# A new plan for a one-core kernel: other assumptions on transfers and small products, and another table of rank amounts

## The chip, the core and the metric

The kernel runs on one NeuronCore of a Trainium2 chip. TensorE (PE) multiplies matrices, VectorE (DVE), ScalarE (ACT) and GpSimd (POOL) work element by element, and SyncE (SP) issues nearly all transfers between the chip's main memory and the core's. Each of these runs its own list of instructions in the order in which they were written, and waits on semaphores where an instruction needs another engine's result. The metric is the device time of one execution in microseconds, the median of three runs.

## What is computed

```python
def reference(**kwargs):
    ...
    attn_out = _attn_ref(**attn_kwargs)
    B, H, S, D = attn_out.shape
    x = np.ascontiguousarray(attn_out.transpose(0, 2, 1, 3)).reshape(B * S, H * D)
    x = _moe_ref(x=x, **moe_kwargs)
    return _moe2_ref(x=x, **moe2_kwargs)

def _attn_ref(r, k, v, w, u):       # batch 4, 8 heads, 768 steps, 48 wide
    for t in range(S):
        kt, vt, rt = (k[:, :, t], v[:, :, t], r[:, :, t])
        cur = np.einsum('bhd,bhe->bhde', u[None] * kt, vt)
        y[:, :, t] = np.einsum('bhd,bhde->bhe', rt, state + cur)
        state = w[None, :, :, None] * state + np.einsum('bhd,bhe->bhde', kt, vt)

def _moe_ref(x, w_in, w_out):       # 3072 tokens, 384 to 2048 to 384
    h = x @ w_in
    sp = np.where(h > 20.0, h, np.log1p(np.exp(np.minimum(h, 20.0))))
    return (h * np.tanh(sp)) @ w_out

def _moe2_ref(x, w_in, w_out, a, b):
    h = x @ w_in
    P = a[0] + a[1] * h + a[2] * h**2 + a[3] * h**3
    Q = 1.0 + np.abs(b[0]) * np.abs(h) + np.abs(b[1]) * h**2
    return (P / (Q + 1e-06)) @ w_out
```

A linear attention with a decaying state is followed by two layers of 384 to 2048 to 384 with an activation between the two products of each.

## The kernel before

The attention is cut into 24 units: 6 chunks of 128 steps for each of 4 batches. A unit (`unit`) loads its keys, receptances and values (`kraw`, `rraw`, `tkv`), multiplies them by powers of the decay `P_T`, and makes a group of small matrix products on PE: the scores (L731), the values (L824, with L818 for the part from the state; L767 in the first two units) and the state's new part (L808; L793 in the first two). In the first four units the diagonal comes from four products two columns wide with the tile `uT` (L708), which holds the input `u`; `uT` is filled by two transfers of single numbers, 0.8 KB each. Two groups (L671) lay out powers of the decay once, and L777 turns the first two units' result round.

Each layer works through 16 slices of 128 features for blocks of 512 tokens. A slice is nine products into a bank `h` (L913), an activation on ACT, DVE and POOL, and nine products into `acc` (L989). A product with 512 columns is full size; the first 24 groups of layer one have 256 columns (half size), so that they may begin when two batches are through the attention. Each value is split into a high and a low part, hence three products for one. Weights come in 64 bits and are brought to 32 bits and split by five or six instructions on ACT, DVE and POOL (L62 to L80, L517, L536).

The order of all this is not written by hand. Everything is recorded as operations in `Plan.ops`, and `Plan.order` makes a list of them when the kernel is built: it keeps a clock for each engine from assumed durations, and picks at each step, among the operations that could start about first, the one of highest rank. A rank is the length of the chain behind an operation plus an amount from the table `PRIO`. Three kinds of assumption bear on the change. A transfer is taken to land `lat` after its last byte, at `move` microseconds of the transfer engines. A group's `rows` says how strongly it is taken to load PE, from which the plan derives the clock that PE is assumed to have. Where the plan finds PE without work in the first 75 us, it puts in fillers: products of zeros into `acc` (L982), which add nothing to the result. They start after eight products of zeros that clear the banks (L650, L978).

Of the kernel before, what the change touches and what calls it, by code (L numbers as in the profile page):

```python
# [18 lines left out]
B, H, S, D = 4, 8, 768, 48  # L19
# [66 lines left out]
def slow_path(tc, nc, d):  # L86
# [133 lines left out]
PRIO = {  # L220
# [32 lines left out]
}  # L253
# [43 lines left out]
class Plan:  # L297
# [72 lines left out]
    def order(self):  # L370
# [14 lines left out]
        for n, x in PRIO.items():  # L385
            self.ops[n].rank += x
        free, clock = {"P": 0.0}, Clock()
        avail = [op for op in self.ops if not op.left]
# [78 lines left out]
def fast_path(tc, nc, d):  # L467
# [3 lines left out]
    pl = Plan()  # L471
# [36 lines left out]
    def dma(dst, src, r=(), w=(), nbytes=196608, after=(), boost=0.0, queue=SP):  # L508

        small = nbytes == 98304  # L510
        return pl.add([(queue, 0.4 if queue != SP else 0.65 if small else 0.5)],
                      lambda e: eng[e].dma_start(out=dst(), in_=src()),
                      r=r, w=w, lat=1.5 if small else 0.757, after=after, move=nbytes / 4.0e5, boost=boost)

# [89 lines left out]
    def setup():  # L604
        dma(lambda: wv(), lambda: d["wT"], w=[wv], nbytes=1000)
        pl.add([(G, 0.1)], lambda e: nc.gpsimd.memset(uT(), 0.0), w=[uT])
        for i in range(2):
            dma(lambda i=i: uT()[64 * i:64 * i + D, :, i], lambda i=i: d["u"].rearrange("(j c) e -> c e j", c=2)[i], w=[uT], nbytes=1000)

# [53 lines left out]
    def powers(after):  # L663

        for i in range(2):
            ps = n_h()

            def ptr(e, i=i, ps=ps):
# [4 lines left out]
                return x_  # L673
            pl.add([(T, 0.9)], ptr, r=[P_T, idn], w=[ps], rows=0.375, after=after)
            pl.add([(A, act(192))],
# [8 lines left out]
    def unit(U):  # L684
# [14 lines left out]
        if U < EARLY:  # L699

            pr = am[0]
            pl.add(mul_opts(512, True), lambda e: eng[e].tensor_tensor(
                out=pr(), in0=kraw(), in1=rraw()[:, :, ::-1], op=ALU.mult), r=[kraw, rraw], w=[pr], boost=bo)
            dp = bank()

            def dsum(e):
                for j in range(4):
                    x_ = nc.tensor.matmul(dp()[:, 2 * j:2 * j + 2], lhsT=pr()[:, j, :], rhs=uT()[:, j, :],  # L708
                                          start=True, stop=True)
                return x_  # L710
            pl.add([(T, 0.75)], dsum, r=[pr, uT], w=[dp], boost=bo, rows=0.2)
            pl.add([(A, 0.2), (V, 0.15)], lambda e: copy(e, dg(), dp()[:, 0:H]), r=[dp], w=[dg], boost=bo)
# [46 lines left out]
        if U < TOK:  # L759
# [3 lines left out]
            def values(e):  # L763
# [5 lines left out]
                return x_  # L769
            pl.add([(T, 1.5)], values, r=[tkv] + am, w=[pv], boost=bo)  # L770
            pl.add([(A, act(384, 0.052)), (V, tt(384), False, VA)],
# [26 lines left out]
        else:  # L798
# [34 lines left out]
            if not last and not join:  # L833
                pl.add([(T, 0.5)], outer, r=[(tkv, 0), (tkv, 1)], w=[kp], boost=bo, rows=0.8)
            xparts = [(xr, i) for i in range(2)]
# [312 lines left out]
```

## Time and profile before

| what | us |
|---|---|
| three runs | 927.40, 928.82, 928.01; median 928.01 |
| profiled execution | 926.85 |
| its span, first to last instruction | 925.1 |
| busy in the span: PE, ACT, DVE, POOL | 908.6, 735.3, 678.9, 525.1 |
| mean granted clock of PE, as a share of 2.4 GHz | 0.989 |

The span is the part of an execution that the profile shows; about 1.8 us of the execution lie outside it. PE busy includes fillers and matmuls that run at the lower clock, so a busy PE is not one that advances at full speed.

### The profile page before, as it was taken

What the parts mean: (1) busy time and instruction counts of PE and PEld (TensorE: products, weight loads), DVE (VectorE), ACT (ScalarE), POOL (GpSimd) and SP (SyncE); (2) the same over time, 40 slices, a digit from 0 to 9 for tenths busy, and PEclk for the clock granted to TensorE, in tenths of its full rate; (3) what the DMA queues carried; (4) which work ended last, traced back from release to release, by engine and by line L of the source; (5) the groups of instructions that cost most, each with busy time, mean ns of one, the idle gap of its engine ahead of it and who ended that gap; (6) DMA issues with size and microseconds to landing.
All of it is one profiled execution on the core that took longest, in us unless ns stands there. A gap on an engine that the chain in (4) does not pass through costs nothing.

```text
span 925.1 us, 14144 instructions
## 1 busy us (share of the span) xinstructions
PE 908.6 (98%) x5094; PEld 750.6 (81%) x5094; DVE 678.9 (73%) x1028; ACT 735.3 (79%) x1310; POOL 525.1 (57%) x468
## 2 busy tenths in 40 slices
PE   7999999999999999999999999999999999999996
PEld 6878778888788888878888888888888888888885
DVE  5699699555545554557868888887877888878894
ACT  4688877767657776769789898997978989878994
POOL 2347747631545421122067597777777876866763
PEclk7899999999999999999999999999999999999999
DMA  8575535230432211117045020020000200100001
GB/s 280 173 262 153 161 122 192 65 123 23 138 95 78 91 46 50 46 49 289 1 140 191 1 68 12 1 69 1 34 24 1 69 12 0 58 1 1 34 1 38
DMA packets 37584, 73.95 MB, mean 80 GB/s; under 512 B 4609, under 2 KB 15746, under 8 KB 37506
## 3 DMA queue, kind: packets, MB, share of 16 engines
q1 hardware_dynamic: 37362, 72.70, 24.1%
q8 instruction: 42, 0.69, 0.3%
q14 instruction: 36, 0.29, 0.1%
q10 hardware_dynamic: 144, 0.26, 0.1%
HBM read 57.61 MB, written 11.01 MB: 74 GB/s over the span
## 4 chain that ended last, share of the span: by engine, by line
PE 91%; DVE 4%; DMA 2%; ACT 2%; issue 1%; POOL 0%; SPq 0%; POOLq 0%; ACTq 0%; DVEq 0%
PE acc L989 41%; PE h L913 32%; PE aps L913 8%; PE aps L731 2%; PE aps L824 2%; PE aps L818 2%; PE acc L982 1%; DVE wr L80 1%; DVE wr L76 1%; DMA uT<-in_u 1%; DMA wr<-in_w 1%; DVE w L536 1%; ACT e L932 1%; PE aps L808 1%; ACT am L748 0%
## 5 line engine op out<-in xcount | busy, mean ns | idle before, releaser
L989 PE MATMUL acc<-gh,w 128*128 128x512 f32 (+1 forms) x1188 | 378.0, 385 | 0.7 <-ACT gh L517 0.7
L913 PE MATMUL h<-xh,w 128*128 128x512 f32 (+1 forms) x960 | 307.0, 384 | 1.8 <-DVE gl L938 1.1
L932 ACT ACTIVATE e<-e 128x512 f32<-128x512 f32 (+1 forms) x408 | 238.1, 602 | 59.1 <-DVE e L928 53.2
L989 PEld LDWEIGHTS acc<-gh,w 128*128 128x128 f32 x1188 | 221.5, 188 | 46.2 <-ACT gh L517 1.1
L989 PE MATMUL acc<-gl,w 128*128 128x512 f32 (+1 forms) x594 | 228.0, 384 | 0.3 <-DVE gl L938 0.2
L913 PEld LDWEIGHTS h<-xh,w 128*128 128x128 f32 x960 | 178.6, 188 | 39.1 <-DVE gl L938 1.1
L913 PE MATMUL h<-xl,w 128*128 128x512 f32 (+1 forms) x480 | 183.4, 382 | 0.4 <-DVE xl L536 0.4
L951 POOL TENSOR_TENSOR v<-v,x 128x512 f32<-128x512 f32 x96 | 124.2, 1300 | 41.7 <-ACT v L945 38.1
L536 POOL TENSOR_TENSOR gl<-yy,gh 128x512 fp32r<-128x512 f32 x94 | 121.7, 1299 | 26.8 <-ACT gh L517 22.2
L989 PEld LDWEIGHTS acc<-gl,w 128*128 128x128 f32 x594 | 111.7, 188 | 22.3 <-DVE gl L938 0.8
L934 DVE SCALAR_TENSOR_TENSOR h<-e,h 128x512 f32<-128x512 f32 (+1 forms) x102 | 67.3, 660 | 57.5 <-ACT e L932 57.3
L913 PEld LDWEIGHTS h<-xl,w 128*128 128x128 f32 x480 | 90.3, 188 | 17.5 <-DVE xl L536 0.6
L928 DVE TENSOR_SCALAR e<-h 128x512 f32<-128x512 f32 (+1 forms) x102 | 66.9, 656 | 48.5 <-PE h L913 48.2
L938 DVE TENSOR_TENSOR gl<-h,gh 128x512 fp32r<-128x512 f32 (+1 forms) x102 | 66.8, 655 | 31.1 <-ACT gh L517 30.1
L517 ACT ACTIVATE gh<-h 128x512 fp32r<-128x512 f32 (+1 forms) x99 | 55.7, 564 | 31.4 <-DVE h L934 31.0
L953 ACT ACTIVATE x<-v,ceps 128x512 f32<-128x512 f32 x96 | 69.0, 723 | 14.1 <-POOL v L951 14.0
L945 ACT ACTIVATE v<-x,cf 128x512 f32<-128x512 f32 x96 | 77.6, 816 | 0.3
L913 PE MATMUL aps<-xh,w 128*128 128x512 f32 x228 | 75.1, 390 | 0.0
L715 POOL TENSOR_TENSOR kraw<-kraw,P_T 128x512 f32<-128x512 f32 x19 | 26.7, 1406 | 55.3 <-DMA kraw<-in_kT 55.3
L963 DVE SCALAR_TENSOR_TENSOR v<-v,ceps,h 128x512 f32<-128x512 f32 x58 | 43.0, 745 | 16.7 <-ACT h L961 16.4
L955 DVE TENSOR_TENSOR yy<-yy,h 128x512 f32<-128x512 f32 x58 | 39.7, 686 | 20.9 <-ACT yy L948 18.8
L913 PEld LDWEIGHTS aps<-xh,w 128*128 128x128 f32 x228 | 42.8, 188 | 8.8
(136 smaller groups left out, 1358.6 us busy)
## 6 DMA issues: line engine op xcount, KB each, us to landing
wr<-in_w SPq DMA_DIRECT2D x32, 768.0 KB, 5.1
tkv<-in_tkv SPq DMA_DIRECT2D x24, 384.0 KB, 3.2
rraw<-in_rT SPq DMA_DIRECT2D x24, 256.0 KB, 3.6
kraw<-in_kT SPq DMA_DIRECT2D x24, 256.0 KB, 2.7
x<-o SPq DMA_DIRECT2D x24, 256.0 KB, 2.3
o<-x SPq DMA_DIRECT2D x24, 256.0 KB, 3.0
out_x<-o SPq DMA_DIRECT2D x17, 256.0 KB, 2.3
xr<-y SPq DMA_DIRECT2D x44, 96.0 KB, 3.4
```

The lines of the kernel that those rows point to most:

```text
L517: return nc.scalar.activation(out=out, in_=x, func=AF.Copy)
L536: lambda e: eng[e].tensor_tensor(out=lo(), in0=x(), in1=hi().bitcast(F32), op=ALU.subtract),
L913: x_ = nc.tensor.matmul(h()[:, :n], lhsT=w()[:, a, m, :], rhs=x()[:, m, col:col + n], start=(i == 0), stop=(i == 8))
L928: pl.add([(V, tt(n))], lambda e: nc.vector.tensor_scalar(out=es(), in0=hp(), scalar1=20.0, scalar2=None, op0=ALU.min), r=[h], w=[e_])
L932: lambda e, func=func, kw=kw: nc.scalar.activation(out=es(), in_=es(), func=func, **kw), w=[e_])
L934: lambda e: nc.vector.scalar_tensor_tensor(out=hp(), in0=es(), scalar=-0.5, in1=hp(), op0=ALU.add, op1=ALU.mult), r=[e_], w=[h])
L938: lambda e: nc.vector.tensor_tensor(out=gls(), in0=hp(), in1=ghs().bitcast(F32), op=ALU.subtract),
L945: lambda e: nc.scalar.activation(out=v(), in_=x(), func=AF.Identity, scale=cf()[:, 5:6], bias=cf()[:, 4:5]), r=[x, cf], w=[v])
L951: lambda e: eng[e].tensor_tensor(out=v(), in0=v(), in1=x(), op=ALU.mult), r=[x], w=[v])
L953: lambda e: nc.scalar.activation(out=x(), in_=v(), func=AF.Ln, bias=ceps()), r=[v, ceps], w=[x])
L963: lambda e: nc.vector.scalar_tensor_tensor(out=v(), in0=v(), scalar=ceps(), in1=h(), op0=ALU.add, op1=ALU.mult), r=[h, ceps], w=[v])
L989: x_ = nc.tensor.matmul(ac[m]()[:, col:col + n], lhsT=w()[:, a, 3 + m, :], rhs=x()[:, :n], start=(first and i == 0 and s > 0), stop=(final ...
```

## The change

The table `PRIO` is replaced: it held other amounts, and now has 409 entries. Six assumptions in the planner are altered: the transfer engines are taken as occupied until 1.8 us, a transfer lands later (`lat` 1.1 for 0.757, and 1.6 for 1.5 on the 96 KB ones) and moves at 0.39 MB per us for 0.4, each half of `uT` counts as 80,000 bytes for 1,000, and five kinds of small product have another duration or load PE less. Nothing else is altered; all products, transfers and element-wise operations are those of before, and only the order, the choice of engine where an operation has one, and the number of fillers differ. Lines after the table stand seven lines further down (L708 is L715, L982 is L989, and L989 is L996).

```diff
--- before.py
+++ after.py
@@ -218,38 +218,45 @@
 PRIO = {
-    21: 17, 29: -1, 31: 384, 39: -30, 41: -150, 43: -213, 53: -152, 54: 84, 56: -56, 59: -47, 60: -2, 66: -8, 67: -5,
...
+    15: 13, 28: -62, 31: -45, 46: 257, 54: -44, 55: -26, 56: -192, 64: -49, 79: 18, 82: -69, 120: -7, 127: -9,
...
@@ -384,7 +391,7 @@
             op.rank = op.boost + max([c + 0.15 + x.rank - x.boost for x in op.succ + places[op]] + [t + x.rank for x, t in op.chain], default=c)
         for n, x in PRIO.items():
             self.ops[n].rank += x
-        free, clock = {"P": 0.0}, Clock()
+        free, clock = {"P": 0.0, "dma": 1.8}, Clock()
         avail = [op for op in self.ops if not op.left]
         order = []
         while avail:
@@ -510,7 +517,7 @@
         small = nbytes == 98304
         return pl.add([(queue, 0.4 if queue != SP else 0.65 if small else 0.5)],
                       lambda e: eng[e].dma_start(out=dst(), in_=src()),
-                      r=r, w=w, lat=1.5 if small else 0.757, after=after, move=nbytes / 4.0e5, boost=boost)
+                      r=r, w=w, lat=1.6 if small else 1.1, after=after, move=nbytes / 3.9e5, boost=boost)
 
     def copy(e, out, x):
         if e == A:
@@ -605,7 +612,7 @@
         dma(lambda: wv(), lambda: d["wT"], w=[wv], nbytes=1000)
         pl.add([(G, 0.1)], lambda e: nc.gpsimd.memset(uT(), 0.0), w=[uT])
         for i in range(2):
-            dma(lambda i=i: uT()[64 * i:64 * i + D, :, i], lambda i=i: d["u"].rearrange("(j c) e -> c e j", c=2)[i], w=[uT], nbytes=1000)
+            dma(lambda i=i: uT()[64 * i:64 * i + D, :, i], lambda i=i: d["u"].rearrange("(j c) e -> c e j", c=2)[i], w=[uT], nbytes=80000)
 
         def small(fn, r, w, e=V, c=0.1):
             pl.add([(e, c)], fn, r=r, w=w)
@@ -671,7 +678,7 @@
                     x_ = nc.tensor.matmul(ps()[:, j * D:(j + 1) * D], lhsT=P_T()[rows, j, :], rhs=idn()[rows],
                                           start=True, stop=True)
                 return x_
-            pl.add([(T, 0.9)], ptr, r=[P_T, idn], w=[ps], rows=0.375, after=after)
+            pl.add([(T, 0.9)], ptr, r=[P_T, idn], w=[ps], rows=0.2, after=after)
             pl.add([(A, act(192))],
                    lambda e, i=i, ps=ps: copy(A, P_t().rearrange("p (j c e) -> p c j e", j=4, c=2)[:, i],
                                               ps()[:, 0:192].rearrange("p (j e) -> p j e", j=4)),
@@ -708,7 +715,7 @@
                     x_ = nc.tensor.matmul(dp()[:, 2 * j:2 * j + 2], lhsT=pr()[:, j, :], rhs=uT()[:, j, :],
                                           start=True, stop=True)
                 return x_
-            pl.add([(T, 0.75)], dsum, r=[pr, uT], w=[dp], boost=bo, rows=0.2)
+            pl.add([(T, 0.75)], dsum, r=[pr, uT], w=[dp], boost=bo, rows=0.05)
             pl.add([(A, 0.2), (V, 0.15)], lambda e: copy(e, dg(), dp()[:, 0:H]), r=[dp], w=[dg], boost=bo)
         ps = [bank(), bank()]
         for x in (kraw, rraw):
@@ -767,7 +774,7 @@
                         x_ = nc.tensor.matmul(pv()[:, h * D:(h + 1) * D], lhsT=am[i]()[:, j, :],
                                               rhs=tkv()[:, 384 + h * D:384 + (h + 1) * D], start=True, stop=True)
                 return x_
-            pl.add([(T, 1.5)], values, r=[tkv] + am, w=[pv], boost=bo)
+            pl.add([(T, 1.6)], values, r=[tkv] + am, w=[pv], boost=bo, rows=0.4)
             pl.add([(A, act(384, 0.052)), (V, tt(384), False, VA)],
                    lambda e: copy(e, yt().rearrange("p (c e j) -> p j c e", c=2, j=4),
                                   pv()[:, 0:384].rearrange("p (j c e) -> p j c e", j=4, c=2)), r=[pv], w=[yt], boost=bo)
@@ -831,7 +838,7 @@
             pl.add([(A, act(512, 0.052)), (V, tt(512), False, VA)],
                    lambda e: copy(e, y()[:, :, :CH], pv().rearrange("p (h t) -> p h t", h=4)), r=[pv], w=[y], boost=bo)
             if not last and not join:
-                pl.add([(T, 0.5)], outer, r=[(tkv, 0), (tkv, 1)], w=[kp], boost=bo, rows=0.8)
+                pl.add([(T, 0.5)], outer, r=[(tkv, 0), (tkv, 1)], w=[kp], boost=bo, rows=0.5)
             xparts = [(xr, i) for i in range(2)]
             for i in range(2):
```

On SP, the first transfers of the program (12 of them, an input's name behind the arrow), before:

```order
L512 DMA tkv<-in_tkv 128x768
L512 DMA wv<-in_wT 128x4
L512 DMA rraw<-in_rT 128x512
L512 DMA kraw<-in_kT 128x512 x2
L512 DMA uT<-in_u 48x4x1
L512 DMA rraw<-in_rT 128x512
L512 DMA wr<-in_w 128x1536
L512 DMA uT<-in_u 48x4x1
L512 DMA wr<-in_w 128x1536 x3
```

and with the change (the first 11):

```order
L519 DMA wv<-in_wT 128x4
L519 DMA uT<-in_u 48x4x1
L519 DMA kraw<-in_kT 128x512
L519 DMA rraw<-in_rT 128x512
L519 DMA wr<-in_w 128x1536
L519 DMA uT<-in_u 48x4x1
L519 DMA rraw<-in_rT 128x512
L519 DMA tkv<-in_tkv 128x768
L519 DMA kraw<-in_kT 128x512
L519 DMA wr<-in_w 128x1536 x2
```

The two transfers of `uT` were the sixth and the ninth, the second of them behind 2,176 KB of others; they are now the second and the sixth, the second behind 1,280 KB. The first keys and receptances move ahead of the first `tkv`.

On PE, from the last products of zeros to the first scores (`aps` and `h` are banks, `acc` the accumulators), before:

```order
L978 MATMUL acc_159<-zer 128x512
L978 MATMUL acc_161<-zer 128x512
L978 MATMUL acc_163<-zer 128x512
L982 MATMUL acc_159<-zer 128x512 x7
L708 MATMUL aps_94<-uT,am 128x2 x4
L982 MATMUL acc_159<-zer 128x512 x2
L731 MATMUL aps_95<-rraw,kraw 128x128
```

and with the change, where three clearings and four fillers stand ahead of these rows:

```order
L657 MATMUL aps_94<-zer 128x512
L657 MATMUL aps_95<-zer 128x512
L657 MATMUL h_96<-zer 128x512
L657 MATMUL h_97<-zer 128x512
L657 MATMUL h_98<-zer 128x512
L989 MATMUL acc_137<-zer 128x512 x11
L715 MATMUL aps_94<-uT,am 128x2 x4
L989 MATMUL acc_137<-zer 128x512 x2
L738 MATMUL aps_95<-rraw,kraw 128x128
```

Between the clearings and the first L708 group (now L715) there were 7 fillers and are 15; the two after it remain.

On PE, from the first unit's values on (two score groups and more stand around this piece), before:

```order
L767 MATMUL aps_95<-tkv,am 128x48 x8
L982 MATMUL acc_159<-zer 128x512 x4
L777 MATMUL aps_94<-idt,tr 128x128 x3
L793 MATMUL aps_95<-tkv 48x48 x8
L982 MATMUL acc_159<-zer 128x512 x2
L767 MATMUL h_98<-tkv,am 128x48 x8
L982 MATMUL acc_159<-zer 128x512
L708 MATMUL aps_94<-uT,am 128x2 x4
L777 MATMUL h_96<-idt,tr 128x128 x3
L793 MATMUL h_97<-tkv 48x48 x8
```

and with the change, from the first turned result to the third score group, and then from the second turned result on:

```order
L784 MATMUL aps_94<-idt,tr 128x128 x3
L800 MATMUL aps_95<-tkv 48x48 x8
L989 MATMUL acc_137<-zer 128x512
L715 MATMUL aps_94<-uT,am 128x2 x4
L774 MATMUL h_98<-tkv,am 128x48 x8
L738 MATMUL aps_95<-rraw,kraw 128x128
```

```order
L784 MATMUL h_96<-idt,tr 128x128 x3
L800 MATMUL h_97<-tkv 48x48 x8
L831 MATMUL aps_95<-am,tkv 48x128 x8
L920 MATMUL h_98<-xh,w 128x256
L920 MATMUL h_98<-xl,w 128x256
L920 MATMUL h_98<-xh,w 128x256 x2
L920 MATMUL h_98<-xl,w 128x256
L920 MATMUL h_98<-xh,w 128x256 x2
L920 MATMUL h_98<-xl,w 128x256
L920 MATMUL h_98<-xh,w 128x256
L815 MATMUL aps_94<-tkv 48x48 x8
L715 MATMUL aps_95<-uT,am 128x2 x4
```

Before, 45 fillers stand behind the first scores: 10 up to the second L767 group and its neighbours, 5 ahead of the first half-size L913 group, and 30 between that and the sixth. With the change 6 stand there: one in the piece shown, two after the third half-size L913 group (now L920), and three single ones. Between the first scores and the first half-size group PE now runs three score groups, L671, two L708 groups, two L767, two L777, two L793 and one L824 with one filler among them.

## Rows read from the trace of the kernel before

**Rows 1.** The page: busy time with share, and PE's granted clock by slice.

```profile
PE 908.6 (98%) x5094; PEld 750.6 (81%) x5094; DVE 678.9 (73%) x1028; ACT 735.3 (79%) x1310; POOL 525.1 (57%) x468
...
PEclk7899999999999999999999999999999999999999
```

**Rows 2.** Stretches: length, busy time (instructions) of each engine, PE's clock, transfers.

```profile
0.00:10.00 10.00, 5.55 (x15) 4.09 (x15) 3.81 (x21) 1.28 (x1) 2.19 (x15) 1.00 0.78 238
10.00:13.00 3.00, 1.73 (x12) 1.40 (x14) 2.63 (x4) 1.53 (x4) 0.88 (x1) 1.00 1.01 416
13.00:30.30 17.30, 17.30 (x102) 15.51 (x101) 9.45 (x16) 11.65 (x27) 3.20 (x3) 0.51 0.59 197
30.30:64.10 33.80, 32.18 (x316) 27.55 (x314) 29.85 (x44) 24.97 (x59) 16.24 (x12) 1.00 0.71 236
64.10:100.00 35.90, 34.87 (x370) 31.25 (x370) 32.69 (x54) 29.69 (x79) 24.40 (x21) 1.00 0.65 200
140.00:918.00 778.00, 778.00 (x4065) 639.21 (x4063) 567.12 (x846) 633.24 (x1085) 453.76 (x395) 1.00 0.18 59
918.00:925.10 7.10, 0.18 (x1) 0.00 (x0) 0.23 (x1) 0.60 (x1) 0.00 (x0) 0.71 0.34 120
```

**Rows 3.** PE's waits: for what, us in total, times, longest.

```profile
PE aps L708 <- DMA uT<-in_u: 3.5, 1, 3.5
...
PE h L913 <- DVE gl L938: 1.1, 2, 0.5
...
PE acc L989 <- DVE gl L938: 0.2, 1, 0.2
```

**Rows 4.** Fillers alone (L982), in three stretches; columns as in Rows 2.

```profile
13.00:30.30 17.30, 4.09 (x8) 2.46 (x9) 0.51 0.59 197
30.30:36.10 5.80, 0.88 (x3) 0.19 (x1) 1.00 0.67 225
36.10:64.10 28.00, 10.01 (x35) 6.14 (x35) 1.00 0.72 239
```

**Rows 5.** Timeline of PE: start, duration, instruction, count, idle before.

```profile
5.78 1.97 PE L982 MATMUL acc<-zer 128*128 128x512 f32 x7
11.27 1.02 PE L708 MATMUL aps<-uT,am 128*128 128x2 f32 x8 [3.52 <-DMA uT<-in_u]
...
12.80 1.91 PE L731 MATMUL aps<-rraw,kraw 48*128 48x128 f32 x16
14.49 2.67 PE L671 MATMUL h<-idn,P_T 48*128 48x48 f32 x16
17.09 1.86 PE L708 MATMUL h<-uT,am 128*128 128x2 f32 x8
...
20.37 2.08 PE L731 MATMUL h<-rraw,kraw 48*128 48x128 f32 x16
22.38 3.65 PE L767 MATMUL aps<-tkv,am 128*128 128x48 f32 x16
...
29.08 0.88 PE L793 MATMUL aps<-tkv 128*48 128x48 f32 x16
...
30.54 1.88 PE L767 MATMUL h<-tkv,am 128*128 128x48 f32 x16
...
32.56 0.95 PE L708 MATMUL aps<-uT,am 128*128 128x2 f32 x8
...
34.60 0.57 PE L793 MATMUL h<-tkv 128*48 128x48 f32 x16
35.10 1.16 PE L731 MATMUL aps<-rraw,kraw 48*128 48x128 f32 x16
...
43.33 0.28 PE L913 MATMUL h<-xh,w 128*128 128x256 f32 x1
...
44.49 1.16 PE L731 MATMUL aps<-rraw,kraw 48*128 48x128 f32 x16
```

**Rows 6.** The tile uT: time from issue to landing of its two transfers.

```profile
DMA to landing us min/median/max: 5.2/5.8/6.4
```

69 rows, old and new, of the table PRIO are left out of this document.

## The prediction

> **What bounds the kernel now.** I read the page first. PE is busy for 908.6 of 925.1 us, no other engine for more than 735.3, and its granted clock is below full only at the start [rows 1]. So the span is PE's own list, and the question is where PE spends time on something other than this list's useful products. The table of stretches answers it [rows 2]: from 140 to 918 us PE is busy in 778.00 of 778.00 us at full clock, so there a new order can win nothing and can only lose by a wait. After 918 come the last copies and the output, 7.1 us, which stay. What can be won lies ahead of 100 us, and is of four kinds. First, PE has run its first fillers by 7.75 us and then waits 3.52 us, until 11.27, for the second transfer of `uT` [rows 5]. Second, 45 further fillers stand behind the first scores; their busy times are 4.09, 0.88 and 10.01 us in three stretches, 15.0 in all [rows 4]. Third, from 13.0 to 30.3 us PE is busy without a gap, yet at a granted clock of 0.51, that is 1.2 instead of 2.4 GHz [rows 2]. Fourth, PE waits in short pieces: behind the long one of 3.5 us there are seven groups of waits on DVE and ACT from 1.1 down to 0.2 us, 3.9 us together (the first and the last are shown) [rows 3].
>
> **What feeds PE there.** DVE is the fullest engine beside PE: 29.85 of 33.80 us between 30.3 and 64.1, and 32.69 of the next 35.90 [rows 2]. Ahead of 30.3 it is busy for only 3.81 + 2.63 + 9.45 = 15.9 us. So the fillers of the middle stretch mostly stand where DVE was late, and a better order must get DVE to work earlier.
>
> **The change, term by term**, against the profiled execution (span 925.1). The useful products are the same, so only the four kinds count.
>
> *Start, -1.5 us.* In the old order 2,176 KB stand ahead of the second `uT` transfer, in the new one 1,280 KB. The slower of the two took 6.4 us to land [rows 6], and PE went on at 11.27. With 0.59 of the bytes ahead I estimate a landing between 7 and 9 us. PE now has 15 fillers instead of 7 in front of the first L708 group. Seven took 1.97 us from 5.78 on [rows 5]; at full clock one costs 10.01 / 35 = 0.29 us busy [rows 4], about 0.25 without the overlap at a run's end, so eight more end near 7.75 + 2.0 = 9.75. The fillers, not the transfer, then set the group's start, 1.5 us earlier. The bounds are 0 (the transfer lands as late as now) and -1.5.
>
> *Fillers, -11.3 us.* Neighbours overlap a little: the scores that start at 20.37 last 2.08, and the next group starts at 22.38 [rows 5]. Taking about 0.12 us for each of 12 runs, the 45 cost 15.0 - 1.5 = 13.5 us. Six remain. At 0.5 us each at the low clock (4.09 / 8 [rows 4]) and 0.25 at the high one, half of them at either, they cost 2.2. The bounds are -11.3 and 0, the latter if PE waits wherever a filler stood.
>
> *Lower clock, +8.4 us.* This is what the removed fillers may cost. The rows give a price for each group at both clocks [rows 5]: scores 2.08 against 1.16 us, values of the first units (L767) 3.65 against 1.88, L708 1.86 against 0.95, L793 0.88 against 0.57. L671 lasts 2.67 and was seen at the low clock only; at most half of it, 1.3, is the clock's. In the old order the first scores (1.91, so 0.75 too much), L671, one L708, one score, one L767 and one L793 group lie in the slow stretch: 0.75 + 1.3 + 0.91 + 0.92 + 1.77 + 0.31 = 6.0 us. Fillers make up 4.1 of the 17.3 us there [rows 4], and the clock comes back right behind six of them. The new order has one filler there. If the clock falls as before, up to the first half-size L913 group the slow stretch holds L671, two L708, two scores, two L767, two L793 and one L824 (priced as scores): 1.3 + 1.8 + 1.8 + 3.5 + 0.6 + 0.9 = 9.9 us. A half-size group takes 1.16 us at full clock (43.33 to 44.49 [rows 5]); at the low clock I estimate 1.1 more. I take the clock to come back with the third such group, since in the old order it came back behind wide products: 9.9 + 1.1 + 0.3 + 0.9 + 1.1 + 0.9 = 14.2, rounded up to 14.4 for part of the third, 8.4 more than before. The bounds are -6.0 (it never falls) and +16.5 (back only with the second half-size L989 group, by the same prices).
>
> *Short waits, +0.5 us.* By the semaphores of the two orders, 82 DVE instructions had to end before the sixth half-size L913 group, and 78 have to now. DVE's need has not grown, but the cushions are gone. I take 4.4 us for 3.9. The bounds are -3.9 and +8, the latter if most of the removed fillers become waits.
>
> Everything later I cost at nothing: from 140 us on PE covers the other engines, the busiest of which (ACT) has 633 of 778 us [rows 2]; if that cover failed, each wait would add its full length. At the end ten L989 groups follow the last L913 group instead of six, so the last activations have more cover than now.
>
> The sum is -1.5 - 11.3 + 8.4 + 0.5 = -3.9 us: span 921.2, execution 922.9 for 926.85. The median of before lies 1.2 above its profiled execution, so I forecast 928.0 - 3.9 = 924.1.
>
> **A rule against the trace.** The stretch from 13.0 to 30.3 us shows PE without a gap at 0.51 of full clock [rows 2]. The Trainium skill ("TensorE: Matmul & The Clock Gate", Part 1, on the HAM clock gate) says that the throttled state is the default and that activity releases it: a PE kept busy runs at 2.4 GHz. By that, the new order, which keeps PE busy from its first product on, would have no slow stretch behind the start. This would give the first rival below. The trace of before disagrees, since busy with small products was not enough there.
>
> **Rivals.** *The clock holds or comes back early.* For it: with 15 fillers PE no longer idles 3.5 us ahead of the first scores, and the fall at 13.0 followed that idling. Against it: the whole slow stretch was busy. With the clock back by the second L767 group the slow part is 1.3 + 0.9 + 1.8 + 0.9 + 0.3 = 5.2 us, so the term is -0.8 and the sum would be -13. But DVE sets a limit: its 45.7 us of work up to 64.1, plus at least the 6.2 that it idles in the first 10 us and some 3 us of transfers and scores that it must await, put the sixth half-size group no earlier than 55 us. So -9, a median of 919.
>
> *Waits take the fillers' place.* The old fillers stood where PE had nothing to do; if DVE is no earlier, each filler removed turns into idle time, and the lower clock hides it in part. For it: DVE at 0.88 and 0.91 of the two busy stretches. Against it: 18 us of DVE idle ahead of 64 us, 14.4 of them ahead of 30.3. With 3 to 5 us of waits above my term the sum is -1 to +1, a median of 927 to 929.
>
> *The low clock lasts (slower).* Products of 48 and 2 columns and only one wide filler leave PE slow through the half-size groups. The sum is zero at 18.3 us of excess: by the prices above, when the clock comes back only after the fourth half-size L913 group. Back with the second L989 group it is -1.5 - 11.3 + 16.5 + 0.5 = +4.2, a median of 932.
>
> **How the numbers follow.** I give the forecast 0.42, the early clock 0.20, waits for fillers 0.20, the lasting low clock 0.18. About 0.2% (1.9 us) is what a measurement of this kernel can tell from no change. Faster by more: 0.60 (the early clock, and all but 0.02 of the forecast); within it 0.22; slower 0.18. The range 918 to 930.5 leaves out the best of the first rival and most of the last, 0.2 together; the forecast's own range is 921 to 926.
>
> **What would show it.** In the new profile the first L715 group starts near 9.8 us, not 11.3; PE's clock reads 0.5 from about 13 to the low forties; the fillers fall to 23; the sixth half-size L920 group starts near 60 us instead of 64; nothing changes from 140 us on. I am wrong at the first term if the group starts past 10.5, at the third if the clock is full before 30 us or still low at 50, at the fourth if PE's waits on DVE and ACT pass 7 us.

## The result, and the profile after

The changed kernel takes 917.38 us (four runs, 917.02 to 918.55) where the kernel before took 927.96 in runs beside it: a ratio of 0.9882, 95% interval 0.9865 to 0.9898. That is 10.6 us less; 3.9 were forecast, and the range ended at 918. The profiled execution took 917.02 us, 9.8 less than that of before, with a span of 915.2. The page of the new kernel, to set beside [rows 1]:

```profile
PE 902.7 (99%) x5063; PEld 745.5 (81%) x5063; DVE 676.8 (74%) x1025; ACT 726.8 (79%) x1295; POOL 536.8 (59%) x477
...
PEclk7699999999999999999999999999999999999999
```

The stretches of the new kernel, with the columns of [rows 2] (cut at 37.2 and 55.7, where its first and sixth half-size groups begin):

```profile
10.00:13.00 3.00, 3.00 (x36) 2.64 (x36) 1.79 (x3) 1.52 (x6) 2.29 (x2) 1.00 1.02 426
13.00:30.30 17.30, 15.39 (x87) 14.09 (x87) 13.63 (x20) 14.73 (x26) 7.21 (x5) 0.50 0.89 326
30.30:37.20 6.90, 6.90 (x60) 6.20 (x59) 6.90 (x10) 3.06 (x5) 3.35 (x2) 0.52 0.50 175
37.20:55.70 18.50, 18.29 (x215) 16.39 (x214) 17.39 (x30) 16.37 (x41) 13.22 (x11) 1.00 0.79 254
140.00:908.00 768.00, 767.52 (x3968) 629.35 (x3967) 557.62 (x830) 614.86 (x1056) 448.28 (x394) 1.00 0.18 58
```

and two stretches of the kernel before, cut where its first and sixth half-size groups stand (37.4 and 64.0), with the one from the start to the first such group, in the kernel before and then in the new one:

```profile
13.00:37.40 24.40, 24.40 (x171) 22.03 (x170) 13.60 (x22) 14.93 (x35) 6.66 (x6) 0.65 0.63 208
37.40:64.10 26.70, 25.08 (x247) 21.02 (x246) 25.70 (x39) 21.70 (x51) 12.78 (x10) 1.00 0.71 236
0.00:37.40 37.40, 31.68 (x196) 27.51 (x197) 20.03 (x46) 17.74 (x38) 9.73 (x21) 0.77 0.70 233
0.00:37.20 37.20, 33.05 (x206) 29.19 (x206) 27.38 (x53) 21.52 (x38) 15.03 (x23) 0.68 0.78 279
```

The column to read first is the third busy time, DVE's. Both kernels reach the first half-size group at about 37.3 us. On the way DVE did 13.60 us of work in the old one, and 13.63 + 6.90 = 20.53 in the new one; from the start on it is 20.03 and 27.38. Behind it the old one needs 25.70 us of DVE in 26.7 us, all that DVE has; the new one 17.39 in 18.5, and its sixth half-size group starts at 55.65 instead of 64.0. DVE is not alone in this: up to the same point ACT did 21.52 us for 17.74, POOL 15.03 for 9.73, and the transfers ran at 279 GB/s for 233. Part of the work that moved is seen on DVE's timeline. Pieces of layer one's weights (L76, L80, and L543, which was L536) stand in the new kernel at

```profile
15.94 0.96 DVE L76 SCALAR_TENSOR_TENSOR wr<-wr 128x768 int32<-128x768 int32 x1
16.81 1.81 DVE L543 TENSOR_TENSOR w<-wr,w 128x768 fp32r<-128x768 f32 x1
18.54 0.95 DVE L80 SCALAR_TENSOR_TENSOR wr<-wr 128x768 int32<-128x768 int32 x1
```

while the kernel before still has such pieces, 5.6 us in these three rows, at

```profile
49.08 1.76 DVE L76 SCALAR_TENSOR_TENSOR wr<-wr 128x768 int32<-128x768 int32 x1
...
56.32 1.77 DVE L536 TENSOR_TENSOR w<-wr,w 128x768 fp32r<-128x768 f32 x1
58.01 2.05 DVE L80 SCALAR_TENSOR_TENSOR wr<-wr 128x768 int32<-128x768 int32 x1
```

The weights are the smaller part of DVE's lead. Up to the first half-size group its weight pieces take 11.0 us for 8.2 (L73, L76, L80 and L543), its attention pieces 13.7 for 8.7 (L709, L722, L745 and L760: keys, receptances, `tkv`, masks). ACT's two weight steps on the 64-bit values (L62 and L71) take 11.7 us for 6.3.

The new kernel's waits, as in [rows 3], and its fillers alone (L989, columns as in [rows 4]):

```profile
PE h L920 <- DVE w L543: 1.2, 1, 1.2
PE aps L784 <- ACT tr L524: 1.1, 1, 1.1
PE aps L715 <- DVE xl L792: 0.8, 1, 0.8
```

```profile
13.00:36.90 23.90, 0.80 (x1) 0.29 (x1) 0.50 0.78 282
36.90:75.00 38.10, 1.92 (x5) 0.88 (x5) 1.00 0.71 224
```

With three more of 0.2 to 0.3 us, PE's waits behind the start are 3.8 us, for 3.9 before. PE's timeline, as in [rows 5]:

```profile
9.43 0.98 PE L715 MATMUL aps<-uT,am 128*128 128x2 f32 x8
...
11.91 1.73 PE L678 MATMUL h<-idn,P_T 48*128 48x48 f32 x16
13.57 1.86 PE L715 MATMUL h<-uT,am 128*128 128x2 f32 x8
15.29 3.63 PE L774 MATMUL aps<-tkv,am 128*128 128x48 f32 x16
18.85 2.08 PE L738 MATMUL h<-rraw,kraw 48*128 48x128 f32 x16
...
31.32 2.08 PE L738 MATMUL aps<-rraw,kraw 48*128 48x128 f32 x16
...
34.91 0.88 PE L800 MATMUL h<-tkv 128*48 128x48 f32 x16
35.59 1.71 PE L831 MATMUL aps<-am,tkv 128*48 128x128 f32 x16
37.23 0.39 PE L920 MATMUL h<-xh,w 128*128 128x256 f32 x1
...
55.65 0.28 PE L920 MATMUL h<-xh,w 128*128 128x256 f32 x1
```

and the clock around its return:

```profile
36.00:37.00 1.00, 1.00 (x14) 1.00 (x11) 1.00 (x3) 0.00 (x1) 0.00 (x0) 0.57 1.01 391
37.00:38.00 1.00, 1.00 (x12) 0.81 (x8) 1.00 (x2) 1.00 (x2) 0.00 (x0) 1.00 1.11 337
```

The scores, values and L715 groups last as long as at the half clock of [rows 5] (2.08, 3.63, 1.86), up to the L831 group. The L920 group behind them runs at full clock.

### The profile page after: what moved, and what is told of

It reads as the page before. It is cut to its first block, busy times and chain, and to the rows that moved or that the text cites. A ratio compares the mean times of both kernels' runs of the same rounds, so it can differ in the third digit from the quotient of the medians.

```text
span 915.2 us, 14064 instructions
## 1 busy us (share of the span) xinstructions
PE 902.7 (99%) x5063; PEld 745.5 (81%) x5063; DVE 676.8 (74%) x1025; ACT 726.8 (79%) x1295; POOL 536.8 (59%) x477
## 4 chain that ended last, share of the span: by engine, by line
PE 90%; POOL 3%; DVE 2%; ACT 1%; DMA 1%; issue 1%; SPq 0%; POOLq 0%; DVEq 0%; ACTq 0%
PE acc L996 41%; PE h L920 33%; PE aps L920 8%; PE aps L738 3%; PE aps L831 2%; PE aps L825 2%; POOL v L958 1%; DMA wr<-in_w 1%; POOL gl L543 1%; PE acc L989 1%; PE aps L815 1%; DMA xr<-y 1%; PE aps L715 0%; POOL w L543 0%; DVE wr L80 0%
## 5 line engine op out<-in xcount | busy, mean ns | idle before, releaser
L996 PE MATMUL acc<-gh,w 128*128 128x512 f32 (+1 forms) x1188 | 378.3, 385 | 0.0
L920 PE MATMUL h<-xh,w 128*128 128x512 f32 (+1 forms) x960 | 307.6, 384 | 1.5 <-DVE w L543 1.2
L996 PEld LDWEIGHTS acc<-gh,w 128*128 128x128 f32 x1188 | 221.2, 188 | 45.0 <-issue 0.2
L996 PE MATMUL acc<-gl,w 128*128 128x512 f32 (+1 forms) x594 | 228.0, 384 | 0.2 <-POOL gl L543 0.2
L920 PEld LDWEIGHTS h<-xh,w 128*128 128x128 f32 x960 | 178.4, 188 | 38.8 <-DVE w L543 1.4
L920 PE MATMUL h<-xl,w 128*128 128x512 f32 (+1 forms) x480 | 183.1, 381 | 0.0
L543 POOL TENSOR_TENSOR gl<-yy,gh 128x512 fp32r<-128x512 f32 x94 | 121.5, 1298 | 19.0 <-ACT gh L524 15.5
L996 PEld LDWEIGHTS acc<-gl,w 128*128 128x128 f32 x594 | 111.6, 188 | 23.0 <-POOL gl L543 0.9
L920 PEld LDWEIGHTS h<-xl,w 128*128 128x128 f32 x480 | 90.3, 188 | 16.9
L920 PE MATMUL aps<-xh,w 128*128 128x512 f32 x228 | 75.5, 390 | 0.0
L962 DVE TENSOR_TENSOR yy<-yy,h 128x512 f32<-128x512 f32 x58 | 39.8, 685 | 18.0 <-ACT yy L955 10.9
L920 PEld LDWEIGHTS aps<-xh,w 128*128 128x128 f32 x228 | 42.8, 188 | 9.5 <-DVE yy L976 0.6
L728 POOL TENSOR_TENSOR tr<-tr,tkv 128x384 f32<-128x384 f32 x20 | 21.3, 1067 | 45.6 <-DMA tkv<-in_tkv 45.6
```

Of the source, the lines that this page charges most:

```text
L543: lambda e: eng[e].tensor_tensor(out=lo(), in0=x(), in1=hi().bitcast(F32), op=ALU.subtract),
L920: x_ = nc.tensor.matmul(h()[:, :n], lhsT=w()[:, a, m, :], rhs=x()[:, m, col:col + n], start=(i == 0), stop=(i == 8))
L996: x_ = nc.tensor.matmul(ac[m]()[:, col:col + n], lhsT=w()[:, a, 3 + m, :], rhs=x()[:, :n], start=(first and i == 0 and s > 0), stop=(final ...
```

## The experiments

The theory after the first reading: in the old order DVE was late behind 37 us, the fillers stood where PE would have waited for it, and the new order's gain is weight work done by DVE ahead of 37 us, which makes them needless. Rivals: the fillers held PE up by themselves; the start; the clock. Orders below are edited behind the planner, so that all other instructions stay in their places. `k` counts fillers. Each run has one trace, of one of its executions; that execution's time is given where it lies far from the median.

**1. The old order without the 30 fillers.**

```diff
-            (self.fill if op in made else op.fn)(op.eng)
+            k += op in made
+            if op in made and 25 <= k <= 54: continue
+            (self.fill if op in made else op.fn)(op.eng)
```

> The old order, with only the 30 fillers between the first and the sixth half-size L913 group left out; every other instruction stands where it stood, and the result is the same. Theory (the fillers stood where DVE was late): DVE is busy in 25.7 of the 26.7 us of that stretch, so the sixth group still starts near 64, PE now waits some 6 to 8 us on DVE there, and the time is within 1 us of before (927 to 929), a little more if the granted clock falls. Rival (the fillers held PE up by themselves): the sixth group starts near 57 and the time is 920 to 922.

Measured: 928.87, ratio 1.0009 (0.9994 to 1.0025), no gain from some 7 us of products left out. The first half-size group starts at 38.28 in this trace, the sixth at 66.66 instead of 64.0. Its waits and its stretches:

```profile
PE h L913 <- DVE w L536: 2.1, 2, 1.8
PE aps L818 <- DVE am L753: 1.8, 1, 1.8
PE aps L808 <- DVE tkv L738: 1.2, 1, 1.2
```

```profile
44.00:51.00 7.00, 7.00 (x41) 6.37 (x41) 4.68 (x11) 4.53 (x13) 5.19 (x5) 0.51 0.97 349
55.70:64.10 8.40, 4.75 (x44) 3.73 (x42) 8.40 (x11) 5.64 (x11) 4.11 (x3) 0.82 0.71 244
62.00:67.00 5.00, 4.73 (x49) 4.22 (x50) 3.67 (x9) 5.00 (x16) 0.94 (x1) 0.50 0.52 147
```

Waits on DVE took the fillers' place (DVE 8.40 of 8.40 us busy, PE 4.75), and behind those that ended at 41.8 and 62.3 us the granted clock was 0.5 for some microseconds, though PE was busy again. In the old order, then, a filler cost nothing: it stood in for a wait and for a stretch at half clock.

**2. The new order with 26 fillers put back** (`more` names the operations behind which they stand).

```diff
+        made, more = set(), {187: 7, 274: 1, 286: 8, 387: 2, 228: 5, 207: 3}
...
+            for i in range(more.pop(op.n, 0)): self.fill(op.eng)
```

> The new order, with 26 fillers put back between the first and the sixth half-size L920 group, where they stood before. Theory (DVE is ahead there now, so PE alone sets the pace): 26 fillers at 0.25 us are 6.5 us, of which the short waits on DVE and ACT take back 1 to 2: the time is 922 to 924. Rival (DVE or a transfer still sets the pace there): the fillers run in idle time and the time stays at 917 to 918.5.

Measured: 923.47, ratio 0.9953 (0.9936 to 0.9970), 6.1 us above the changed kernel, or 0.23 for each filler; its sixth half-size group starts at 61.70 instead of 55.65. Its stretch of 37.2 to 55.7:

```profile
37.20:55.70 18.50, 18.50 (x175) 16.05 (x172) 13.78 (x27) 14.54 (x34) 11.03 (x10) 0.99 0.75 238
```

In the new order a filler has its full price: PE sets the pace there, and DVE (13.78 of 18.5) has room.

**3. The old order with an early `uT`**: operations 2 and 3, its two transfers, stand right behind operation 1.

```diff
+        made, order = set(), [op for op in self.order() if op.n not in (2, 3)]
+        i = order.index(self.ops[1]) + 1
+        for op in order[:i] + self.ops[2:4] + order[i:]:
```

> The old order, with only the two transfers of uT moved ahead on SP (now the fourth and fifth transfer instead of the sixth and ninth). Theory (the start term of the prediction, and DVE setting the pace from there on): uT has landed by 8 us, the first L708 group starts between 8 and 9.5 instead of 11.27, DVE's work behind it moves with it, and the time is 1.5 to 3 us less (925 to 926.5). Rival (the start is hidden because DVE waits for other things before 37 us): the first group starts earlier, but the first half-size group does not, and the time is within 0.7 us of before.

Measured: ratio 0.9991 (0.9976 to 1.0006). The first group starts at 7.78 instead of 11.27, and yet the first half-size one at 38.05, not ahead of the 37.45 of before:

```profile
7.78 1.02 PE L708 MATMUL aps<-uT,am 128*128 128x2 f32 x8
...
12.27 1.46 PE L731 MATMUL aps<-rraw,kraw 48*128 48x128 f32 x13 [1.72 <-ACT dg L517]
...
38.05 0.28 PE L913 MATMUL h<-xh,w 128*128 128x256 f32 x1
```

The rival's result holds: 3.5 us at the start are gone by 37 us. Its reason holds in part: PE waits 0.7 us for `rraw` and 1.7 for `dg` ahead of the first scores, and then the clock, full there before, reads 0.50 again from 33.2 to 36.6 us. PE's early start alone is worth less than can be measured; the interval leaves room for 2.2 us.

**4. The new table up to operation 599 only**, with the old table's amounts behind and the new assumptions.

```diff
-PRIO = { ... }
+PRIO = {the new amounts of operations below 600, the old ones of all others}
```

> The changed kernel with the new table only for operations numbered below 600 (73 of its amounts: the set-up, the first units and the first half-size slices) and the old table's amounts for all others; the assumptions are the new ones. Theory (all of the gain lies ahead of the sixth half-size group): PE's order is the same up to there, and the time is 917 to 919. Rival (the later amounts contribute): 921 to 925.

Measured: 932.38, ratio 1.0046 (1.0028 to 1.0063): both were wrong, and the kernel is 15 us slower than the changed one. Up to the sixth half-size group it is the changed kernel (55.66 us). It loses in layer two, ahead of the second activation (`yy`):

```profile
PE aps L920 <- DVE yy L976: 5.1, 1, 5.1
PE h L920 <- DVE yy L976: 3.1, 2, 2.8
```

```profile
875.00:880.00 5.00, 1.21 (x6) 0.66 (x4) 4.12 (x7) 4.64 (x8) 3.44 (x4) 0.96 0.00 0
880.00:885.00 5.00, 3.64 (x9) 2.90 (x10) 5.00 (x8) 0.49 (x1) 0.62 (x1) 0.50 0.01 2
```

So the early amounts bring the early gain, and with the old later ones it is lost again: PE waits 8.2 us on `yy`, and the clock is halved behind the wait. I had costed all behind 140 us at nothing. That came out so (767.52 of 768.00 us busy), but ACT's 633 of 778 us, my reason, is none: here ACT is no fuller and PE waits.

**5. The old order, weight pieces early, fewer fillers.** `MOVES` holds 18 pairs; the first of a pair is put ahead of the second in the list. Nine are DVE's, eight ACT's and one SP's (the expectation counts 11 and 6 in error).

```diff
+MOVES = [(80, 48), (98, 48), (104, 48), (81, 254), (85, 254), (86, 254), ...]
...
+        for n, m in MOVES:
+            order.remove(self.ops[n])
+            order.insert(order.index(self.ops[m]), self.ops[n])
+        for op in order:
+            k += op in made
+            if op in made and 25 <= k <= 54: continue
```

> The old order with two edits: 18 instructions of the weights' preparation (11 on DVE, 6 on ACT, 1 transfer) move ahead of instructions at which DVE and ACT idled between 24 and 37 us, and the 30 fillers between the first and the sixth half-size L913 group are left out (as in the run with fewer fillers, which alone gave +1). Theory (the gain is DVE's weight work done in its idle time, which makes the fillers needless): with some 6 us of DVE work gone from the stretch of 37 to 64, the sixth half-size group starts near 58 instead of 64 and the time is 921 to 924. Rival (DVE's lead does not matter, or the clock falls without fillers): 927 to 930.

**6. The same moves with all 54 fillers.**

> The old order with only the first of those two edits: the same 18 instructions earlier, all 54 fillers kept. Theory: PE's own list, the fillers in it, now sets the pace; only the waits of some 2 us between 44 and 64 can go: 925.5 to 927.5. Rival (the gain comes from DVE alone): the same 921 to 924 as with both edits.

Measured: ratios 0.9977 (0.9961 to 0.9993) and 0.9977 (0.9962 to 0.9991), 2.1 us each. The sixth run has the theory's time. PE's waits behind the start fall from 3.9 to 1.4 us; from 37.2 on PE has no gap, and DVE is busy for 12.64 of 18.5 us:

```profile
37.20:55.70 18.50, 18.50 (x188) 16.23 (x184) 12.64 (x24) 14.27 (x36) 9.98 (x9) 0.95 0.71 238
```

From its first to its sixth half-size group it takes 23.95 us (40.75 to 64.70) instead of 26.55; but in this trace the first came 3.3 us later than before, the clock reading 0.50 from 11.8 us on. The fifth run lies between its two ranges: 30 fillers fewer gave nothing more. In its trace, of an execution of 928.16 with a median of 925.84, the sixth group starts at 64.69, not at 58, and one wait stands out (lines stand ten further down here):

```profile
PE h L923 <- DVE gl L948: 4.4, 2, 3.8
```

DVE idled 3.29 us for `gh` there; ACT reached `gh` only after an L62 that had waited 2.54 us for a transfer of weights. So in this execution DVE's queue was not the limit: the next link, the transfers' place on SP, was late too. Where the run's 2.1 us were won, this execution does not show.

**7. The new order with eight fillers more near 21 us** (as in 2, with `more = {62: 8}`).

> The new order, with eight fillers more behind the second score group (near 21 us, in the stretch at half clock). They cost 3.5 us at the half clock, 1 of it in a wait that is there. Theory (from 13 to 37 us DVE, busy for 20.5 of 24 us, sets the pace nearly as much as PE, so the half clock costs far less than its prices): the clock may come back near 25, the first half-size group does not start more than 1 us earlier, and the time is 917 to 919. Rival (the half clock costs what the prices say, some 0.4 us per us at it): the first half-size group starts 2 to 4 us earlier and the time is 913.5 to 915.5. If the clock does not come back: 919 to 920.

Measured: 917.72, ratio 0.9890 (0.9872 to 0.9908), the same as the changed kernel. Its clock:

```profile
20.00:28.00 8.00, 6.14 (x49) 5.02 (x48) 7.58 (x12) 7.57 (x14) 4.92 (x3) 0.93 0.92 328
28.00:38.00 10.00, 9.52 (x66) 8.07 (x66) 10.00 (x13) 6.30 (x10) 3.88 (x3) 0.50 0.65 231
```

In this trace the clock also fell later, at 17.6 us, so it was full for some 10 us more than in the changed kernel's. The first half-size group came 1.1 us earlier, the sixth 0.7, the end not at all. DVE and ACT are busy for 7.58 and 7.57 of the 8 us from 20 on, and PE for 6.14: a faster PE waits there, 1.9 us of it on DVE's `xl`.

**8. The new order with the L80 of 28.0 us done five times.**

```diff
+            for i in range(5 if op.n == 93 else 1): (self.fill if op in made else op.fn)(op.eng)
```

> The new order, with the DVE instruction of 28.0 us (L80, whose result doesn't change when it is repeated) done five times: 3.5 to 3.8 us more of DVE work. Theory (DVE is nearly full from there to 56 us and its lead is what the gain rests on): the groups behind it start 1.5 to 3.5 us later, PE waits on DVE for as much, and the time is 919 to 921. Rival (PE sets the pace alone, DVE has a reserve of several us): less than 1 us, 917 to 918.5.

Measured: 921.59, ratio 0.9939 (0.9916 to 0.9962), 4.2 us more. The five took 5.65 us where one takes 0.95, so 4.7 us of DVE were added, not 3.6. In the trace, of an execution of 923.44, the first half-size group starts at 42.57, 5.3 later, of which 1.2 were lost ahead of the added work; the half clock lasts to 45:

```profile
29.26 5.65 DVE L80 SCALAR_TENSOR_TENSOR wr<-wr 128x768 int32<-128x768 int32 x5
...
30.30:37.20 6.90, 4.87 (x29) 4.49 (x30) 6.80 (x8) 2.62 (x6) 1.08 (x2) 0.50 0.06 22
37.20:45.00 7.80, 6.83 (x53) 5.45 (x53) 7.62 (x10) 4.42 (x8) 3.07 (x3) 0.50 0.69 246
```

What DVE loses between 28 and 37 us the kernel loses nearly in full. With 2 (PE paces behind 37 us) this is the theory's core: DVE up to there, PE from there on. Ahead of 28 us it is not shown. From 13.0 to 30.3 ACT is fuller than DVE in the new kernel (14.73 and 13.63 of 17.3 us), PE's longest wait there is on ACT (`tr`, 1.1 us), and no run made ACT slower.

**9. The old order, 21 moves, fewer fillers.** Sixteen of the pairs of 5, some with a new place, and five more: `(131, 401)`, a weight transfer earlier on SP, `(102, 193)`, `(109, 383)`, `(132, 231)` and `(133, 294)`; `(94, 69)` and `(95, 74)` are left out.

> The old order without the 30 fillers between the first and the sixth half-size L913 group, and with 21 moves instead of the 18 of the earlier run: fewer pieces of the weights stand ahead of what the first half-size group needs, DVE's later pieces of the fourth and fifth weight (L536) move up, so that SP can issue the next weight's transfer earlier, and ACT's step on that transfer (L62) no longer stands ahead of gh. Theory (the gain needs the whole chain of a weight, transfer, ACT and DVE, to be early; the earlier run freed DVE and then waited 3.9 us behind a transfer): the sixth half-size group starts at 58 to 61, and the time is 921 to 924. Rival (in this order something else always takes the fillers' place): 925 to 928.

Measured: ratio 0.9965 (0.9945 to 0.9985), 3.2 us less, at the lower edge of the rival's range. The trace is of an execution of 928.41, with a median of 925.38. In it the sixth group starts at 63.40, not at 58 to 61; the wait behind `gh` is gone, but PE idles 2.4 us on DVE's `tkv`, and the clock falls behind it:

```profile
40.00:42.00 2.00, 0.00 (x0) 0.00 (x0) 2.00 (x4) 1.94 (x5) 0.00 (x0) 1.00 0.12 39
...
44.00:51.00 7.00, 7.00 (x39) 6.55 (x39) 2.80 (x7) 4.49 (x12) 5.17 (x5) 0.50 0.99 394
```

DVE is free there (2.80 of 7.00): in this execution the pieces put forward pushed `tkv` back, and the half clock cost more. A third of the gain could be had by hand; that the remainder is the same cause was not shown by building it up.

**10. The new order without 12 fillers**: seven of the 15 at the start, and the five behind 37 us.

> The new order without 12 of its 23 fillers: seven of the 15 at the start and the five between the first half-size group and 75 us. Theory (PE sets the pace from 37 us on, so the five cost 1.2 us; the seven held the first L715 group up by 1.7 us, but DVE sets the pace behind it, and the old order's run with an early uT gained next to nothing from 3.5 us): 915.5 to 917. Rival (the fillers there hold the clock or fill waits that are there anyway): 917 to 920.

Measured: 918.08, ratio 0.9885 (0.9858 to 0.9912), as the changed kernel. The median is the rival's, but the interval, some 915 to 920 us, does not tell the two ranges apart. In the trace, of an execution of 920.93, the first L715 group waited 1.8 us for `uT`, until 10.40: the transfer had taken 7.1 us to land, where in the changed kernel the fillers and the transfer (6.1) ended nearly together.

**11. The table alone** (old assumptions) and **12. the assumptions alone** (old table; among them are four kinds of small product, as in the diff of the change, not five).

> Only the table of amounts from the change, the six old assumptions. The plan then holds 73 fillers instead of 23, some 30 of them between the first and the sixth half-size group. Theory (an order is as good as the DVE work that it puts ahead of 37 us and the fillers that it can then leave out; the table gives that order only with the assumptions it was searched under): 925 to 933. Rival (the table is what gains): 917 to 920.

> Only the six assumptions from the change, the old table. The plan holds 70 fillers, some 37 of them between the first and the sixth half-size group. Theory: as with the table alone, 925 to 933. Rival (the assumptions are what gains): 917 to 920.

Measured: 965.30, ratio 1.0381 (1.0333 to 1.0429), and 949.82, ratio 1.0234 (1.0197 to 1.0270). Neither part gains, and both lose far more than I expected. With the table alone the first half-size group starts at 35.34 us, but the sixth at 62.22, with 33 fillers between them; so most of the early gain is gone too:

```profile
62.22 0.28 PE L920 MATMUL h<-xh,w 128*128 128x256 f32 x1
```

With the assumptions alone it starts at 62.44. The plans hold 73 and 70 fillers, busy for 22.3 and 19.1 us, and PE waits 32.1 and 20.4 us in all (9.6 in the kernel before, 6.0 in the changed one), 9.7 and 8.2 of them on `yy` in layer two. The 8.2 us are the waits of run 4 again (5.1 and 3.1), which has the same new assumptions and old later amounts; the old table under its own assumptions has none. So the old later amounts do not fit the new assumptions, and run 4 does not show that the new later amounts gain by themselves.

## Why the prediction was wrong

The faster sign was right and the size was not. Against the profiled execution (-9.8 us) its terms measure:

- *Start*, -1.5 forecast: -1.8 (11.27 to 9.43). The estimate of 9.75 was good. Its worth is another matter: run 3 gave PE twice as much and gained nothing that can be measured, so this term belongs to PE's list and not to the time by itself.
- *Fillers*, -11.3 forecast: six remain, busy for 0.80 + 1.92 us, 2.2 without the overlaps, as forecast. That no waits took their place was the forecast's bet; run 1 shows that in the old order they would have, run 2 that in the new one they don't.
- *Short waits*, +0.5 forecast: 3.8 us for 3.9, so -0.1.
- *Lower clock*, +8.4 forecast: **this is the step that failed.** I took the clock to come back with the third half-size L913 group. It came back at 36.9, during the L831 group and ahead of the first. The groups at half clock by the forecast's own prices [rows 5]: two L715 groups 2 x (1.86 - 0.95) = 1.8; two scores 2 x (2.08 - 1.16) = 1.8; two values 2 x (3.63 - 1.88) = 3.5; two L800 groups 2 x (0.88 - 0.57) = 0.6; L831, priced as scores, 1.71 - 1.16 = 0.6; L678, half of it ahead of 13.0, 0.3. The sum is 8.6 instead of 14.4, and against the 6.0 of before the term is +2.6.

That is -1.8 - 11.3 + 2.6 - 0.1 = -10.6 on PE's list, where -9.8 was measured. Of the 0.8 between them, 0.5 are the L784 groups, for which the forecast had no price (1.65 us each; in the kernel before 1.48 and 1.31), and the rest is within the estimates for overlaps. The medians differ by 0.8 more than the profiled executions, because that of after lies 0.4 above its profile and that of before 1.1.

Behind the size is an error of kind: the term added the half clock's whole price, as if PE set the pace from 13 to 37 us. Run 7 had some 10 us of it back for nothing, and run 8 showed DVE's work there at nearly its full price. The forecast's own sign for this term (full before 30 us, or low at 50) was too wide to show the error. The early-clock rival had its number nearly right (919) by luck, for a reason that didn't occur: the clock read 0.50 from 13.0 to 36.9. It fell there although PE had been busy without a gap since 2.24 us, so the idling ahead of the first scores, to which that rival put the fall, was not needed for it. The limit that it took from DVE's work, the sixth half-size group no earlier than 55 us, is where that group came (55.65, behind 44.8 us of DVE's work and 10.9 of its idle time, for 45.7 and 9.2); it was the better forecast. The waits rival described the old order (run 1), the lasting low clock no run.

PE was busy for 15.39 + 6.90 of 24.2 us at 0.50 to 0.52. So the Trainium skill's rule ("TensorE: Matmul & The Clock Gate", Part 1) that a busy PE runs at full clock does not describe this start: the trace of after disagrees as that of before did.

**What stays open.** Experiments show the two ends: in the old order the fillers cover DVE's lateness, in the new one nothing is left to cover. By moving the old order's weight work I got 3.2 of the 10.6 us, so the early DVE work is shown to be needed from 28 to 37 us (run 8), and early weight work to help (runs 6 and 9), not to be all of it. Those runs moved weight pieces alone, and the larger part of DVE's lead in the new order is attention work; no run moved that. ACT's earlier weight steps, the places of transfers and of `tkv` may belong to it too, and were not told apart.

## What to carry to other kernels

A filler or a busy engine says nothing of its price: take it out of the old order and put it into the new one, and see in which of them it costs time. Where one engine is late, cost a change by that engine's work ahead of the point where it becomes full, and see what kind of work it is before you move any; a price per group at a lower clock counts only in stretches that the clocked engine paces. A searched order is one piece: a part of the table, the table without its assumptions, or the assumptions without the table was 0.5 to 3.8% slower than the old one whole.

## What the runs showed of the hardware

A wait of PE can cost more than its length. In run 9 PE idled from 39.8 to 42.2 us, and the granted clock then read 0.50 from 43 to 53 with PE busy without a gap. In run 1 the same followed a wait of 1.2 us that ended at 41.8; there the clock also fell during a wait of 1.8 us that ended at 62.3, and in run 4 during one of 5.1 us that ended at 881.4, in layer two, and stayed low behind it. A score group then takes 2.08 us instead of 1.16. Not every wait did this: behind the changed kernel's wait of 1.2 us on `w`, after 55.7 us, the clock stays at 1.00.

Executions differ in when the clock falls at the start. In run 7's trace, ahead of its extra fillers, PE's clock was full until 17.6 us, where the changed kernel, with the same instructions up to there, read 0.50 from 13.0 on; runs 4, 8 and 2, with the same instructions too, lie at 12.6, 15.1 and 17.1. And the second `uT` transfer, issued at 3.2 us in each, landed 5.5 to 7.1 us later over the traces of the new order. One trace is one sample of each.
